# One core's linear attention with a four-expert MoE: a new hand-written order for the first two token tiles, 17 filler groups for five, and one q piece moved from GpSimd to VectorE

## The chip, the core and the metric

The kernel runs on one core of a Trainium2 chip. The core has five engines that run side by side, each through its own instructions in a fixed order: TensorE (PE in the profile, and PEld for its weight loads), VectorE (DVE), ScalarE (ACT), GpSimd (POOL) and SyncE (SP). SP, ACT and POOL also issue the DMA transfers of this kernel. An engine stops at an instruction until the semaphores that it waits for are set, and whatever stands behind it on the same engine waits with it.

The metric is the device time of one execution in microseconds (us). The runs of the kernel before gave 484.59, 484.69 and 487.03; the median is 484.69.

## What is computed

```python
def phi(x): return np.where(x > 0, x, np.exp(x) - 1.0) + 1.0
# q, k, v: 8 batches x 8 heads x 576 rows x 64, fp32
kv  = einsum('bhsd,bhse->bhde', phi(k), v)
z   = sum(phi(k), axis=2)
x   = (phi(q) @ kv) / (phi(q) @ z + 1e-6)      # linear attention
x   = x.transpose(0, 2, 1, 3).reshape(4608, 512)
p   = domain_probs / (domain_probs.sum(-1) + 1e-9)
out = sum over 4 experts e of p[:, e] * (relu(x @ w1[e]) @ w2[e])
# w1[e]: 512 x 1024, w2[e]: 1024 x 512
```

The result has 4608 x 512 numbers in fp32. Nearly all of the arithmetic lies in the two layers of the four experts.

## The kernel before

The 4608 tokens go through the experts in nine tiles of 512. Tile j takes 512 of the 576 rows of batch j; the ninth tile gathers the 64 rows that each batch leaves over. Attention of a batch has to be done before its tile can enter layer 1, so the batches behind the first are prepared while PE works on the experts of the tile ahead of them. Only batch 0 has nothing ahead of it.

The kernel writes the order of its instructions itself. Every piece of work is a generator with a name, put into a list with a position. `CFG["EARLY"]` is a list of names written by hand; `advance` (L1126) takes them one by one and runs the generator of that name up to its next `yield`, which emits its instructions. A name stands as often in the list as its generator has parts. What EARLY does not name follows in the order of positions. EARLY covers batch 0, the whole of tile 0, the preparation of batch 1 and most of tile 1. As each engine runs its instructions in the order in which they were emitted, EARLY is the order of all engines and of the DMA queues.

The names that the change and the prediction touch:

- `lq`, `lk`, `lv` load the four pieces of q, k and v of batch 0 (L568, L560). k and v pieces hold two heads with all their rows; q piece i holds half of the heads and half of the rows. A piece is 256 or 288 KB. There are three slots for raw q, so `lq1` waits until one is free.
- For phi: `qe` and `ke` are the exps on ACT (L601, L583), `ql` and `kl` compute max(x + 1, 1) (L604, L586), `qm` and `km` the minimum of both on DVE (L607, L590). CFG["QL"] names the engine of each `ql`, V for DVE and P for POOL.
- `vc` casts v to fp16 (L593); by CFG["VC"] = 'PVAP' pieces 0 to 3 are cast on POOL, DVE, ACT and POOL.
- `qT` transposes q on PE (L615) and copies it on ACT (L617). `kv` is the product of k and v (L626, 18 matmuls for a pair of heads) and two copies into kvz (L637, on ACT or DVE). `nd` computes numerators and denominators (L648) and divides on DVE (L651, L652). `xT` transposes the result (L662) and copies it (L664).
- `L` is one part of expert 0's layer 1 for tile 0 (L675) with its ReLU on ACT (L684).
- `warm` emits fillers (L1016): matmuls of zeros, 128x512, whose result nobody reads. CFG["WARM"] gives the number of matmuls in each `warm`.
- `w1er` and `w2er`, such as w131 or w231, load half r of expert e's weights for layer 1 or 2 (L247 and L241, 512 KB; expert 0's layer 1 comes in four quarters of 256 KB, L244). All of them are issued by POOL. `k0` to `q3` load pieces of batch 1 (L339), and `rk`, `rv` half of its left-over rows (L317), also on POOL. `b1.loadlq` loads the left-over rows of q on SP, in two transfers of 64 KB, and `b1.load1` another k piece ahead of them.
- `p1` to `p7` and `c22` are block products of layer 1 of the other experts and tiles, in Strassen-Winograd form (L887): p1.021 is tile 0, expert 2, half 1. They need the sums of weight blocks `s` (DVE, L765 to L771) and of x blocks `ts` (L868; ts0 on DVE, ts1 and later ones on POOL).
- `ye.xx` is a quarter of layer 2 of expert e for 128 tokens of tile 0 (L735); `m` are the layer 2 products of the later tiles (L830), `hs` and `t` the sums that they need (POOL L797 to L803, DVE L782 to L788).

A POOL weight load has to wait for the landing of the load eight places ahead of it in POOL's own row of loads; in the trace POOL stands still for this several times between 18 and 43 us.

Of the kernel before, what the change touches and what calls it, by code (L numbers as in the profile page):

```python
# [91 lines left out]
    "LV": 'SSSS',  # L92
    "KL": 'VVVV',
    "VC": 'PVAP',
    "QL": 'VVPV',
    "QT": 'AAAA',
    "KC": ('AA', 'AV', 'VA', 'AA'),
    "XT": ('AA', 'AA', 'AV', 'AV'),
    "CUT": (((0, 2, 4),) * 4, ((0, 2, 4),) * 4),
    "MOVE": {"m73.10": 512.0, "m73.11": 512.0, "m73.20": 512.0, "m73.21": 512.0, "m72.41": 528.0},  # L100
    "WARM": (14, 3, 2, 1, 5),
    "BANK": {'qT0': 'py', 'qT1': 'b', 'nd00': 'py', 'nd00+': 'b', 'kv2': 'py', 'xT00': 'b', 'kv3': 'b', 'nd10+': 'b', 'L00': 'b', 'L10': 'py', 'nd01': 'b', 'xT01': 'py', 'nd11+': 'b', 'L20': 'e', 'L30': 'e', 'L01': 'e', 'L11': 'py', 'L21': 'py', 'L31': 'b', 'b1.qT3': 'py', 'b1.nd30': 'py', 'b1.nd21': 'b', 'b1.q1': 'b', 'b1.qT1': 'py', 'b1.nd01': 'py', 'b1.xT2': 'b', 'b1.nd11': 'py', 'b1.xT0': 'b'},
    "EARLY": (
# [31 lines left out]
    ),  # L135
}

# [1032 lines left out]
```

## Time and profile before

| | us |
|---|---|
| median of three runs | 484.69 |
| profiled execution | 484.06 |
| its span, first to last instruction | 482.3 |
| around the span | 1.8 |
| PE busy | 474.5 (98%) |
| PEld busy (overlaps PE) | 407.4 (84%) |
| DVE busy | 377.6 (78%) |
| POOL busy | 356.1 (74%) |
| ACT busy | 331.4 (69%) |

The profile is one execution, taken by the hardware profiler. A row of a timeline gives the start in us from the span's beginning, the time that the instruction or the run of instructions took, the engine, the line of the kernel, the operation, the tile it writes and the tiles it reads, sizes, and how many instructions are in the run (x8). In brackets stands the idle time of the engine just before it and what ended that idle time: [0.49 <-DVE vpos L593] means that the engine stood still for 0.49 us until DVE had written vpos at line 593. Instructions of one engine overlap by some tens of ns up to 0.2 us, so the time from one start to the next is the price of one in a row, and not the time that it took itself.

A row of the busy time by stretches gives the stretch, its length, then for PE, PEld, DVE, ACT and POOL the busy time with the number of instructions, the granted clock of TensorE (1.00 is full), the mean busy share of the core's DMA engines, and GB/s.

### The profile page before, as it was taken

To read this page: it belongs to the slowest core of one execution; us is meant where nothing else is said; L and a number is where in the kernel's file an instruction comes from. 1 tells how busy PE (TensorE), PEld (TensorE's weight loads), DVE (VectorE), ACT (ScalarE), POOL (GpSimd) and SP (SyncE) were. 2 spreads that over 40 slices of the span, in tenths; PEclk is the share of its full clock that TensorE was granted. 3 is DMA by queue.
4 is the path that set the end of the run, shared out by engine and by line. 5 is a ranking of instruction groups with operands and counts; after the bars stand their busy time and mean duration, and the time that the engine had idled before them with its cause. 6 is when DMAs were issued, how large, how long until landed. Compare 5 with 4: busy or idle time off the path is not lost.

```text
span 482.3 us, 12013 instructions
## 1 busy us (share of the span) xinstructions
PE 474.5 (98%) x4565; PEld 407.4 (84%) x4565; DVE 377.6 (78%) x794; ACT 331.4 (69%) x662; POOL 356.1 (74%) x340
## 2 busy tenths in 40 slices
PE   7999999999999999999999999999999999999997
PEld 3766766898889888998889888988898888888886
DVE  5778988997868895889679885988787756775677
ACT  4689989956895599649874888478954465446540
POOL 5566044789866986789777977697769877987775
PEclk9999999999999999999999999999999999999999
DMA  8999986442445154533552436323230020003002
GB/s 292 219 218 256 232 212 210 124 112 83 135 140 115 39 160 154 119 59 117 173 134 62 112 123 170 78 73 112 65 68 12 2 88 2 0 1 89 2 1 87
DMA packets 80025, 53.67 MB, mean 111 GB/s; under 512 B 45088, under 2 KB 72736, under 8 KB 79968
## 3 DMA queue, kind: packets, MB, share of 16 engines
q1 hardware_dynamic: 69920, 40.56, 30.6%
q0 software_dynamic: 8800, 11.27, 12.1%
q10 hardware_dynamic: 1248, 1.08, 0.7%
q8 instruction: 35, 0.57, 0.5%
q14 instruction: 22, 0.18, 0.1%
HBM read 45.16 MB, written 9.44 MB: 113 GB/s over the span
## 4 chain that ended last, share of the span: by engine, by line
PE 96%; DVE 1%; DMA 1%; issue 0%; ACT 0%; SPq 0%; DVEq 0%
PE py L830 39%; PE pb L887 25%; PE pe L887 19%; PE py L735 6%; PE ph L675 1%; PE psum_nd L492 1%; PE psum_kv L464 1%; DMA rawq<-in_q_dram 1%; PE pb L830 1%; PE pe L830 1%; DVE kpos L586 0%; PE psum_nl L510 0%; PE psum_num L648 0%; PE psum_xh L662 0%; DVE qp L607 0%
## 5 line engine op out<-in xcount | busy, mean ns | idle before, releaser
L726 DVE SCALAR_TENSOR_TENSOR acc<-py,p_sb,acc 128x256 f32<-128x256 f32 (+1 forms) x382 | 182.3, 489 | 42.3 <-PE py L830 38.3
L871 DVE CUSTOM_DVE_ANT_0 h<-pe,u 128x512 f16<-128x512 f32 x140 | 96.2, 689 | 45.5 <-PE pe L887 27.8
L887 PEld LDWEIGHTS <-w 128*128 128x128 f16 x1120 | 108.9, 98 | 16.2
L797 POOL TENSOR_TENSOR hs<-h 128x512 f16<-128x512 f16 x64 | 74.6, 1165 | 56.9 <-DVE h L871 52.8
L830 PEld LDWEIGHTS <-h 128*128 128x128 f16 x1024 | 99.6, 98 | 11.5
L830 PE MATMUL py<-w,h 128*128 128x256 f16 x744 | 106.4, 273 | 0.0
L898 ACT COPY u<-pb 128x512 f32<-128x512 f32 x140 | 82.5, 592 | 29.9 <-PE pb L887 27.8
L799 POOL TENSOR_TENSOR hs<-hs,h 128x512 f16<-128x512 f16 x64 | 73.9, 1155 | 26.3 <-PE py L830 23.8
L887 PEld LDWEIGHTS <-s 128*128 128x128 f16 x840 | 81.2, 98 | 12.0 <-DVE s L767 0.2
L887 PE MATMUL pb<-tt,w 128*128 128x256 f16 x560 | 83.9, 273 | 0.0
L830 PEld LDWEIGHTS <-hs 128*128 128x128 f16 x768 | 74.5, 98 | 8.8 <-issue 0.2
L803 POOL TENSOR_TENSOR hs<-h,hs 128x512 f16<-128x512 f16 x64 | 74.4, 1162 | 0.9 <-PE py L830 0.7
L830 PE MATMUL py<-t,hs 128*128 128x256 f16 x496 | 74.1, 273 | 0.0
L801 POOL TENSOR_TENSOR h<-h 128x512 f16<-128x512 f16 x64 | 73.9, 1154 | 0.1
L920 ACT ACTIVATE h<-pe 128x512 f16<-128x512 f32 x70 | 42.0, 601 | 41.3 <-PE pe L887 40.7
L913 ACT COPY pe<-pb 128x512 f32<-128x512 f32 x70 | 40.0, 572 | 42.0 <-PE pb L887 15.8
L941 ACT ACTIVATE h<-pb 128x512 f16<-128x512 f32 x70 | 41.9, 601 | 6.0 <-PE pb L887 5.9
L887 PE MATMUL pe<-tt,s 128*128 128x256 f16 x280 | 42.0, 273 | 0.0
L887 PE MATMUL pb<-tt,s 128*128 128x256 f16 x280 | 41.8, 273 | 0.0
L887 PE MATMUL pe<-xT,s 128*128 128x256 f16 x248 | 37.1, 273 | 0.0
L887 PE MATMUL pb<-xT,w 128*128 128x256 f16 x248 | 37.1, 273 | 0.0
L830 PE MATMUL py<-w,hs 128*128 128x256 f16 x248 | 37.0, 273 | 0.0
(132 smaller groups left out, 594.4 us busy)
## 6 DMA issues: line engine op xcount, KB each, us to landing
w<-in_moe_w_dram POOLq DMA_DIRECT2D x14, 512.0 KB, 10.6
out_dram<-acc SPq DMA_DIRECT2D x28, 256.0 KB, 2.6
rawb<-in_k_dram SPq DMA_DIRECT2D x24, 256.0 KB, 3.0
rawb<-in_q_dram SPq DMA_DIRECT2D x24, 256.0 KB, 2.7
rawb<-in_v_dram SPq DMA_DIRECT2D x24, 256.0 KB, 2.7
out_dram<-acc SPq DMA_DIRECT2D x12, 128.0 KB, 2.4
w<-in_moe_w_dram POOLq DMA_DIRECT2D x4, 256.0 KB, 5.5
rawb<-in_k_dram POOLq DMA_DIRECT2D x4, 256.0 KB, 10.4
```

Source lines behind the costliest of these rows:

```text
L726: nc.vector.scalar_tensor_tensor(out=acc, in0=ps, scalar=pscal, in1=acc, op0=AO.mult, op1=AO.add)
L797: nc.gpsimd.tensor_tensor(out=hs[0], in0=a21, in1=a22, op=AO.add)
L799: nc.gpsimd.tensor_tensor(out=hs[1], in0=hs[0], in1=a11, op=AO.subtract)
L801: nc.gpsimd.tensor_tensor(out=a21, in0=a11, in1=a21, op=AO.subtract)
L803: nc.gpsimd.tensor_tensor(out=hs[3], in0=a12, in1=hs[1], op=AO.subtract)
L830: nc.tensor.matmul(out=ps, lhsT=lhsT(k), rhs=rhs[:, k], start=first and k == 0, stop=k == FH - 1, skip_group_check=True,)
L871: nc.vector._custom_dve(TENSOR_ADD_SAT, out=out, in0=ps, in1=u, s0=BIG, s1=0.0)
L887: nc.tensor.matmul(out=ps[:, kk], lhsT=lk(kc), rhs=rhs[:, kc], start=first and kk == 0 and kc == 0, stop=kc == 1, skip_group_check=True,)
L898: nc.scalar.copy(u, self.b)
L913: nc.scalar.copy(self.e5, self.b)
L920: nc.scalar.activation(self.h[:, :, 0, 0:NH], self.e5, AF.Relu)
L941: nc.scalar.activation(self.h[:, :, 1, 0:NH], self.b, AF.Relu)
```

## The change

Three entries of CFG are altered, and nothing else.

QL gives the third q piece's `ql` to DVE instead of POOL. WARM turns five filler groups with 25 matmuls into one group of 13 and 16 single ones, 29 in all. EARLY goes from 713 to 736 names in a new order. At its head ql3, ql2, qe3, qe2, qm3 and qm2 now come ahead of the work on piece 0; the weight loads w110 to w211 are named sooner among the steps of batch 0; and w231 stands behind w230 and ts1.0, in the rows in which tile 1's first products stand.

POOL's loads in the order in which they are issued:

```
before: w100 w102 w103 w101 w110 w111 k3 w200 rk1 w201 v0 rv0 rk0 v1 rv1 w120 w121 w210 w211 v2 k0 k2
        q1 k1 v3 q0 w130 w131 q3 w220 q2 w221 w231 w230
after:  w100 w102 w101 rv0 w103 w110 w111 w200 rk1 w201 rk0 k3 k2 w120 w121 k1 k0 w210 v2 w211 rv1 v1 v0
        q0 q1 v3 w130 w131 w220 w221 q3 q2 w230 (ts1.0) w231
```

DVE's operations from the first q piece on, by line of the kernel before, with the piece:

```
before: 604 q0, 604 q3, 607 q0, 586 k0, 590 k0, 607 q2, 586 k1, 590 k1, 607 q3, 593 v1, 586 k2, 586 k3, 637, 651, 652, 590 k2, 590 k3
after:  604 q3, 604 q2, 607 q3, 607 q2, 604 q0, 586 k0, 607 q0, 586 k1, 590 k0, 593 v1, 590 k1, 586 k2, 586 k3, 637, 590 k2, 590 k3, 651, 652
```

On POOL the L604 of q2 is gone. On ACT the exps of q3 and q2 stand ahead of that of q0, where those of q2 and q3 stood between and behind the exps of k0 and k1. On PE the first rows are, before: 14 fillers, qT0, 3, qT2, 2, kv0, 1, kv1, nd01, 5; after: 13 and 5 fillers, qT0, 2, qT2, 3, kv0, 2, kv1, 2, nd01, 2, nd00.

The diff, with the first six rows of EARLY and those that name w130 to w231 or p1.101:

```diff
-    "QL": 'VVPV',
+    "QL": 'VVVV',
...
-    "WARM": (14, 3, 2, 1, 5),
+    "WARM": (13,) + (1,) * 16,
...
-        "lq2 lq3 lq0 lk0 qe0 ql0 ql3 qm0 kl0 lk1 lpr0 ke0 km0 qe2 ql2 qm2 lv0 ke1 kl1 km1 warm0 qT0 lv1 lk2 qe3 qm3 warm1 qT2 qT0 vc0 w100 warm2 kv0 vc1 qT2",
-        "warm3 kv1 lk3 kv0 kv0 kl2 kv1 kl3 w102 kv1 nd01 lv3 nd01 warm4 xT11 xT01 ke2 km2 qT3 w103 vc3 lv2 ke3 vc2 nd00 w101 km3 xT01 w110 xT11 w111 kv3 k3 kv2",
-        "qT3 lq1 nd00 qe1 xT00 w200 kv3 rk1 ql1 kv3 kv2 w201 qm1 L01 kv2 nd11 xT10 L31 qT1 v0 nd11 rv0 xT00 xT10 L10 xT21 rk0 xT21 v1 xT31 L11 qT1 xT31 nd10",
-        "L01 L01 rv1 L31 w120 nd10 ts0.2 L00 ts0.0 xT30 ts0.1 xT20 L31 s0.0 L20 xT20 L30 xT30 L10 L10 L00 L00 L30 ts0.3 L30 p1.011 s1.0 p1.010 L11 L20 p1.010",
-        "p2.010 s1.1 L20 w121 p2.010 p1.011 L21 L21 L21 s1.2 p6.010 p5.010 w210 L11 s1.3 p6.011 y0.30 p2.011 p6.010 p7.010 w211 p7.010 s0.1 p6.011 c22.010 v2",
-        "y0.31 y0.00 p4.010 p2.011 y0.32 y0.33 p5.011 b1.k3 k0 pr0 y0.33 t0.0 t0.1 b1.km3 p7.011 p7.011 c22.011 y0.01 y0.02 y0.03 p4.010 b1.lk y0.20 y0.03 k2",
...
-        "s2.1 p2.020 s2.3 s2.2 y0.23 b1.v1 q0 t0.2 p6.020 p6.020 y0.13 p6.021 y0.13 y1.20 p7.020 y1.21 p2.020 p5.020 p7.020 w130 p2.021 y1.22 y1.23 t1.0 y1.10",
-        "w131 p5.021 b1.v2 q3 b1.lkm y1.11 p6.021 b1.k0 b1.k2 b1.k1 w220 t1.1 t1.2 p7.021 y1.12 p7.021 c22.020 p3.020 y1.23 b1.v3 b1.km0 p4.020 p4.020 y1.00",
...
-        "p1.030 b1.qm1 b1.qT1 y1.32 y1.03 b1.qm0 s3.0 p1.031 w231 b1.qT0 s3.1 p2.030 y1.33 p6.030 b1.kv b1.qT0 p6.031 p2.031 b1.nd00 b1.nd01 b1.q3 p6.030 s3.3",
...
-        "b1.xT1 p3.030 b1.nd21 y2.03 b1.xT0 b1.nd20 b1.nd21 y2.23 y2.10 y2.11 ts1.0 p1.101 p1.101 b1.load5 t1.3 b2.load0 t2.0 b1.xT2 y2.12 y2.13 b1.xT2 b2.k1",
...
+        "lq2 lq3 warm0 ql3 ql2 lk0 qe3 qe2 lq0 qe0 qm3 qm2 ql0 lk1 lpr0 lv0 kl0 qm0 kl1 ke0 ke1 lv1 warm1 km0 warm2 warm3 warm4 warm5 qT0 warm6 lk2 warm7 qT2",
+        "vc0 warm8 warm9 warm10 w100 lk3 lv3 w102 w101 rv0 vc3 w103 vc1 km1 w110 w111 kv0 qT2 warm11 w200 rk1 w201 rk0 k3 k2 w120 w121 kl2 k1 k0 w210 kl3 lv2",
+        "v2 w211 rv1 v1 v0 q0 q1 v3 warm12 w130 ke2 lq1 kv1 warm13 kv0 kv0 ke3 kv1 qT0 vc2 warm14 kv1 nd01 warm15 km2 km3 nd01 warm16 nd00 qT3 kv2 xT11 qT3 qe1",
+        "xT01 nd00 xT10 kv3 xT11 xT01 ql1 qm1 kv2 xT00 L11 L01 kv2 xT10 kv3 kv3 nd11 nd11 L21 qT1 xT00 L00 xT31 xT21 xT21 xT31 L20 qT1 nd10 ts0.2 nd10 ts0.0",
+        "s1.0 ts0.1 L01 L11 L01 L21 xT20 L31 xT30 xT20 xT30 L30 L30 L00 L21 L30 L00 L31 L31 L20 p1.011 p1.011 L20 p1.010 s1.1 ts0.3 s1.2 L10 p2.011 s1.3 pr0",
+        "s0.0 p1.010 L10 p2.010 p2.011 L11 L10 p5.011 p2.010 p6.011 p6.010 p6.011 p6.010 y0.20 y0.21 y0.30 p7.010 p5.010 p7.010 b1.lk y0.31 p7.011 y0.22 y0.32",
+        "p4.010 y0.23 p7.011 t0.0 c22.010 w131 w220 y0.33 b1.k2 p4.010 p3.010 y0.23 c22.011 b1.lkm p3.010 p3.011 p4.011 p3.011 y0.33 p4.011 s2.0 s2.1 s2.2 s2.3",
...
+        "b1.xT3 y2.10 p1.101 y2.11 t2.0 b1.qTl b1.load5 b2.load0 w230 ts1.0 w231 b2.lk b1.xT2 p1.100 b1.xT3 b2.k0 p1.101 ts1.1 ts1.2 b2.ones ts1.3 b2.load4",
...
```

45 rows, old and new, of the table nl are left out of this document.

## The prediction

> **What bounds the kernel now.** I read first the busy time by stretches, then what PE waited for, then the timelines of DVE, ACT, POOL and PE up to 75 us.
>
> ```profile
> 8.00:12.00 4.00, 2.71 (x49) 1.42 (x48) 3.90 (x8) 2.81 (x8) 3.98 (x6) 1.00 1.09 367
> 12.00:16.00 4.00, 2.99 (x62) 2.04 (x62) 3.20 (x9) 3.17 (x8) 4.00 (x7) 1.00 1.24 205
> ...
> 24.00:120.00 96.00, 96.00 (x856) 73.63 (x855) 82.81 (x164) 79.92 (x163) 55.42 (x58) 1.00 0.80 182
> 120.00:478.00 358.00, 358.00 (x3489) 320.48 (x3488) 277.49 (x592) 237.22 (x469) 286.72 (x258) 1.00 0.30 82
> ```
>
> After the length of each stretch come PE, PEld, DVE, ACT and POOL busy, then the granted clock, the DMA share and GB/s. From 24 to 478 us PE is busy without a gap and at full clock. The change leaves PE's real matmuls as they are, so it can win time only before about 17 us, where PE waits or runs fillers, and it can lose time wherever a new order makes PE wait.
>
> ```profile
> PE psum_qT L615 <- DVE qp L607: 1.4, 2, 0.7
> ...
> PE psum_num L648 <- DVE kvz L637: 0.8, 1, 0.8
> PE psum_kv L626 <- DVE vpos L593: 0.5, 1, 0.5
> PE psum_xh L662 <- DVE x_sb L652: 0.3, 1, 0.3
> ```
>
> Four links of PE's start wait for DVE, 1.4 + 0.8 + 0.5 + 0.3 = 3.0 us in all. DVE itself:
>
> ```profile
> 6.22 0.76 DVE L604 TENSOR_SCALAR qp<-rawq 128x512 f16<-128x512 f32 x2 [3.71 <-DMA rawq<-in_q_dram]
> 6.90 0.42 DVE L607 TENSOR_TENSOR qp<-ee,qp 128x512 f16<-128x512 f16 x1
> 7.23 0.45 DVE L586 TENSOR_SCALAR kpos<-kraws 128x576 f16<-128x576 f32 x1
> 7.79 0.94 DVE L590 TENSOR_TENSOR kpos<-kexp,kpos 128x576 f16<-128x576 f16 x1
> 8.66 0.41 DVE L607 TENSOR_TENSOR qp<-ee,qp 128x512 f16<-128x512 f16 x1
> 8.99 0.57 DVE L586 TENSOR_SCALAR kpos<-kraws 128x576 f16<-128x576 f32 x1
> 9.66 0.46 DVE L590 TENSOR_TENSOR kpos<-kexp,kpos 128x576 f16<-128x576 f16 x1
> 10.04 0.42 DVE L607 TENSOR_TENSOR qp<-ee,qp 128x512 f16<-128x512 f16 x1
> 10.37 0.75 DVE L593 CAST vpos<-vraws 128x576 f16<-128x576 f32 x1
> 11.04 1.33 DVE L586 TENSOR_SCALAR kpos<-krawt 128x576 f16<-128x576 f32 x2
> 12.40 0.23 DVE L637 CAST kvz<-psum_kv 64x65 f16<-64x65 f32 x1
> ...
> 13.27 0.69 DVE L652 TENSOR_TENSOR x_sb<-psum_num,recip 128x512 f16<-128x512 f32 x1
> 13.88 0.81 DVE L590 TENSOR_TENSOR kpos<-kexp,kpos 128x576 f16<-128x576 f16 x2
> ```
>
> It idles 3.71 us for the first raw q and then has no gap from 6.22 to 12.6 us. Each link that PE waits for stands somewhere in this row of operations.
>
> **The change at the start.** Pieces 2 and 3 of q, which DVE now handles behind piece 0, come first in the new order. That they land before 6.22 is seen on POOL, which begins piece 2 at 4.33 the moment its load is there:
>
> ```profile
> 4.33 1.92 POOL L604 TENSOR_SCALAR qp<-rawq 128x512 f16<-128x512 f32 x1 [2.90 <-DMA rawq<-in_q_dram]
> 7.76 0.66 POOL L593 CAST vpos<-vraws 128x576 f16<-128x576 f32 x1 [1.50 <-DMA vraws<-in_v_dram]
> ```
>
> ```profile
> 6.22 0.63 ACT L601 ACTIVATE ee<-rawq 128x512 f16<-128x512 f32 x1 [3.06 <-DMA rawq<-in_q_dram]
> ```
>
> So three operations leave DVE's gapless row for its idle time: the second L604 (0.34, half of 6.22 to 6.90) and two L607 (0.33 each, 8.66 to 8.99 and 10.04 to 10.37), 1.00 us together. The L604 that QL takes from POOL (1.92 there, 0.34 on DVE) lies in the idle 3.71 as well. ACT loses two exps from its run that begins at 6.22 (0.63 each) into its own idle 3.06.
>
> In the new order DVE runs from 6.22: L604 0.34, L586 0.34, L607 0.33, L586 0.57, so L590 of k piece 0 starts at 7.80, as before, and ends its slot at 8.67. Behind it now come the cast of v piece 1 (0.67, 10.37 to 11.04) to 9.34, L590 of piece 1 (0.38) to 9.72, two L586 (1.36) to 11.08 and L637. So L637 starts 1.3 us sooner than 12.40. Then both L590 of the later pieces (0.81) stand ahead of L652, which stood ahead of them: L637's 0.2 and 0.81 bring L652's pair to about 12.1, where the 13.03 to 13.27 of before becomes 12.1 to 12.3. The first x_sb is 1.0 us sooner. I take **-1.1** for PE's start, between 1.0 and 1.3. The bounds: -0.3, if only the last of the four waits goes, because L590 of k piece 0 does not move; -1.9, if besides the 1.00 that L590 loses its excess (0.94 - 0.46 = 0.48, it runs beside POOL's cast at 7.76) and the links on ACT follow with another 0.4.
>
> On that L590: by the Trainium skill, SBUF — State Buffer, Who interferes with whom, a DVE operation with two SBUF inputs and a GpSimd operation that reads SBUF exclude each other, and whoever is first holds on for its whole length. If DVE is first by a hair in the new order, L590 is 0.48 shorter and POOL's cast later instead, which the sum would carry as -1.5 rather than -1.1. The row 7.79 0.94 beside 9.66 0.46 fits it.
>
> **Fillers.** 25 become 29, five groups become one of 13 and 16 singles.
>
> ```profile
> 11.18 0.48 PE L626 MATMUL psum_kv<-vpos,kpos 64*64 64x65 f16 x18 [0.49 <-DVE vpos L593]
> ...
> 12.85 1.24 PE L1016 MATMUL warm_ps<-qz 128*128 128x512 f16 x5
> ```
>
> One costs 0.23 us (12.85 to 14.02 for five, the row behind it starts there), four more 0.9. I cost them at 0: the 3.0 us of waits cover them, the last of them stands ahead of the first nd00, and what PE waits for comes from DVE. Without that cover they cost 0.9.
>
> On their spread: by the Trainium skill, TensorE: Matmul & The Clock Gate, Part 1, the clock falls to half after a window of some 3.4 us with too little work. By the Trainium skill that would cost here some 2 us of matmuls at half speed, if singles were too thin. The row 8.00 to 12.00 shows PE busy 2.71 of 4.00 with clock 1.00, and in the new order 13 and five singles stand ahead of the first transposes, so I give it nothing.
>
> **Expert weights of layer 1.** POOL's DMA order changes: expert 2's and 3's pieces move, and four b1 pieces pass expert 1's. All pieces are one stream, near 210 GB/s from 24 to 60 us:
>
> ```profile
> GB/s 292 219 218 256 232 212 210 124 112 83 135 140 115 39 160 154 119 59 117 173 134 62 112 123 170 78 73 112 65 68 12 2 88 2 0 1 89 2 1 87
> ```
>
> The tightest piece of before is expert 3's second half of layer 1 (w131). DVE waits for its landing until 51.74, PE reads it at 52.48:
>
> ```profile
>   DMA w<-in_moe_w_dram: 1.0, 1
> ```
>
> ```profile
> 51.74 0.69 DVE L765 TENSOR_TENSOR s<-w 128x1024 f16<-128x1024 f16 x1
> ```
>
> ```profile
> 52.48 0.60 PE L887 MATMUL pe<-xT,w 128*128 128x256 f16 x4
> ...
> 60.83 1.03 PE L735 MATMUL py<-w,h 128*128 128x512 f16 x4
> ...
> 71.75 0.59 PE L735 MATMUL py<-w,h 128*128 128x512 f16 x2
> ```
>
> The same POOL pieces stand ahead of w131 in both orders, so it cannot land sooner. Two 64 KB pieces of left-over q on SP now come before it, since the k pieces that free their way are handled sooner: 128 KB at 218 GB/s is 0.60 us, landing 51.65 + 0.60 = 52.25 (I put the landing 0.1 ahead of 51.74). Counted in the two orders, PE has one group of four 128x256 matmuls more ahead of it (0.43). PE wants it at 52.48 - 1.1 + 0.43 = 51.81: a stall of **+0.44**, that is, at most 0.66 of the 1.1 pass this point (bounds 0 without the two pieces, 1.3 with -1.9 won before). w221 follows with one piece between: 52.25 + 2 x 2.4 (512 KB at 218 GB/s) = 57.1, and is wanted at 60.83 - 0.66 - 2.85 (work that moved behind it) = 57.3: no stall.
>
> **Expert 3's last piece, w231.** Before, POOL issues it as the last of three, by 47.5; now ts1.0 (L868), which waits for tile 1's x, stands ahead of it:
>
> ```profile
> 45.19 2.29 POOL L241 DMA_DIRECT2D w<-in_moe_w_dram  x3
> 64.36 1.16 POOL L868 TENSOR_TENSOR tt<-xT 128x512 f16<-128x512 f16 x1 [16.89 <-ACT xT L536]
> ```
>
> So it is issued at 64.36 + 1.16 - 0.66 = 64.9. No row shows a 512 KB piece with an empty queue. From below, 256 KB took 5.5 (first row); from above, L247 took 6.7 at least and L241 8.9 at least (the rows behind it):
>
> ```profile
> w<-in_moe_w_dram POOLq DMA_DIRECT2D x4, 256.0 KB, 5.5
> ```
>
> ```profile
> DMA to landing us min/median/max: 6.7/8.6/10.5
> ```
>
> ```profile
> DMA to landing us min/median/max: 8.9/12.9/17.3
> ```
>
> It lands at 70.4 to 73.8, by 6.7 at 71.6. I take 6.7, as its queue is shorter than that of any of these. PE reads it first at 71.75 in before and, with 0.12 more work ahead, at 71.87 less what is still won. So this piece lets 0.3 of the win pass.
>
> **Small stalls.** ACT and DVE have little air where the order is new:
>
> ```profile
> 50.00:60.00 10.00, 10.00 (x92) 7.64 (x90) 9.58 (x23) 9.81 (x22) 0.00 (x0) 1.00 1.20 229
> ```
>
> ACT 9.81 and DVE 9.58 of 10.00 while PE is never stopped: a different order costs between 0 and, with three misses of one 128x512 step on ACT (0.4 us, the spacing of PE's groups), 1.2. I take **+0.4** up to w231, where 0.3 of the win may pass anyway, and **+0.2** behind it in tile 1's layer 2.
>
> **Sum.** -1.1 + 0.44 + 0.4 = -0.26 at w231, whose bound (-0.3) then costs nothing; +0.2 behind it: -0.06. Profiled execution 484.06 (span 482.3 and 1.8 around it) to 484.0. The median of before, 484.69, lies 0.63 above that execution; with it the forecast is **484.6**, no change.
>
> **Rivals.** (a) The win stays: no stall at w131 and w231, because the two q pieces or the shorter queue cost less than I put. Then 484.69 - 1.1 = 483.6, with -1.9 482.8. For it: PE's four waits are real. Against: w131's wait on DVE in before shows the stream at its limit. (b) Slower: w231, issued behind ts1.0, takes as long as L241's rows. Landing at 64.9 + 8.9 = 73.8 costs 73.8 - 71.87 = 1.9, with the median 12.9 it costs 5.9: 486.6 to 490.6. It decides once the piece lands behind 71.9. For it: every L241 row; against: those had four pieces ahead. (c) The change does not do what it says: L590 of k piece 0 stays at 7.8, and with it every later link; 0.3 won, 0.4 + 0.2 and no w131 stall: 485.0.
>
> **How the numbers follow.** My forecast 0.40, (a) 0.22, (b) 0.20, (c) 0.18. About 0.5%, 2.4 us, is what a measurement of this kernel can tell from no change: 482.3 to 487.1. Faster beyond that needs more than -1.9: 0.05. Slower needs (b) with more than 9.4 us: 0.16, and 0.03 for stalls of several kinds: 0.19. Same 0.76. The range goes from (a)'s end, 482.8, to (b) with 9.7 us, 487.4; the forecast's own is 483.6 to 485.6.
>
> **What would show it.** In the changed kernel's profile: L604 on DVE at about 4.4 twice; L637 on DVE near 11.1; the first layer 1 matmul 1.0 sooner; a PE wait of about 0.4 for w131 near 52; POOL's w231 issue near 65 and its first reader near 71.6. I am wrong if PE waits for w231 longer than 1 us, if the first x_sb isn't sooner, or if PE shows waits of over 1 us on ACT or DVE behind 24 us.

## The result, and the profile after

The changed kernel takes 487.60 us (median of 13 runs, 487.39 to 489.00) beside 484.68 for the kernel before on the same chips (13 runs); the ratio is 1.0055, 95% interval 1.0043 to 1.0067. The forecast was 484.6 with a range from 482.8 to 487.4, so the time lies above the range. The profiled execution took 487.54 with a span of 485.8, 3.5 more than the span of before.

The busy time by stretches of the changed kernel, in the columns of before (length, PE, PEld, DVE, ACT, POOL, clock, DMA share, GB/s):

```profile
8.00:12.00 4.00, 3.69 (x59) 2.09 (x58) 2.83 (x8) 3.37 (x9) 4.00 (x6) 1.00 1.08 370
12.00:16.00 4.00, 2.88 (x62) 2.19 (x61) 3.44 (x9) 2.47 (x7) 4.00 (x7) 1.00 1.24 212
24.00:120.00 96.00, 93.78 (x825) 70.47 (x824) 82.18 (x160) 76.62 (x154) 52.80 (x54) 1.00 0.79 174
120.00:478.00 358.00, 357.89 (x3486) 320.09 (x3484) 276.53 (x590) 241.21 (x478) 287.71 (x259) 1.00 0.31 84
```

Between 24 and 120 us PE now stands idle for 2.2 us, where it had no idle time at all. What PE waited for, in us altogether, times, longest:

```profile
PE pe L888 <- DVE h L872: 1.9, 2, 1.2
...
PE psum_xh L663 <- DVE x_sb L653: 1.1, 2, 0.6
PE psum_qT L616 <- DVE qp L608: 0.7, 1, 0.7
PE psum_num L649 <- DVE kvz L638: 0.3, 1, 0.3
```

The waits of the start shrank from 3.0 to 2.1 us. A new one stands at the top: PE waits for DVE's relu-and-add (h, L872), which frees the PSUM bank of an expert product. The lines of the changed kernel are one further on than those of before.

To see where the time went, one needs PE's waiting and its fillers together. The table gives, at a moment t, t less the work that PE has done by then; the work is the sum of the usual spacings (0.11 us for a 128x256 matmul, and so on) of the real matmuls begun, taken from the traces. A number that grows by 0.4 from one row to the next means 0.4 us lost between them. The runs e7 and e11 are told below.

```
t (us)   before   changed   e7      e11
 16      14.12    13.48     13.36   13.46
 28      14.30    14.26     13.62   13.60
 50      14.85    14.81     14.17   14.14
 65      14.88    14.82     14.69   14.37
 80      15.33    15.88     15.27   14.96
 85      15.47    16.09     15.28   14.97
 95      15.53    17.49     15.34   15.03
105      15.54    18.61     15.35   15.04
140      16.14    19.73     15.95   15.64
```

The changed kernel is 0.64 us ahead at 16 us and has given this back by 28. It is level with before until 65 us, loses 0.6 by 80, 2.5 from there to 105 and 0.5 by 140.

### The profile page after: what moved, and what is told of

Read it like the earlier page. It is cut to its first block, busy times and chain, and to the rows that moved or that the text cites. A ratio compares the mean times of both kernels' runs of the same rounds, so it can differ in the third digit from the quotient of the medians.

```text
span 485.8 us, 12015 instructions
## 1 busy us (share of the span) xinstructions
PE 476.6 (98%) x4569; PEld 407.5 (84%) x4569; DVE 377.9 (78%) x795; ACT 332.7 (68%) x662; POOL 355.7 (73%) x339
## 3 DMA queue, kind: packets, MB, share of 16 engines
q0 software_dynamic: 8800, 11.27, 12.1%
## 4 chain that ended last, share of the span: by engine, by line
PE 90%; DVE 3%; DMA 3%; ACT 2%; issue 0%; POOL 0%; DVEq 0%
PE py L831 38%; PE pb L888 24%; PE pe L888 18%; PE py L736 4%; DMA w<-in_moe_w_dram 2%; PE ph L676 1%; PE psum_nd L493 1%; DMA krawt<-in_k_dram 1%; PE psum_kv L465 1%; DMA rawq<-in_q_dram 1%; PE pb L831 1%; DVE h L872 1%; PE pe L831 1%; DVE w L789 1%; DVE acc L727 0%; DVE t L787 0%
## 5 line engine op out<-in xcount | busy, mean ns | idle before, releaser
L727 DVE SCALAR_TENSOR_TENSOR acc<-py,p_sb,acc 128x256 f32<-128x256 f32 (+1 forms) x382 | 181.6, 488 | 44.3 <-PE py L831 37.1
L872 DVE CUSTOM_DVE_ANT_0 h<-pe,u 128x512 f16<-128x512 f32 x140 | 95.8, 687 | 46.6 <-PE pe L888 26.3
L888 PE MATMUL pe<-xT,w 128*128 128x256 f16 x248 | 37.1, 273 | 0.0
```

Source lines behind the costliest of these rows:

```text
L727: nc.vector.scalar_tensor_tensor(out=acc, in0=ps, scalar=pscal, in1=acc, op0=AO.mult, op1=AO.add)
L872: nc.vector._custom_dve(TENSOR_ADD_SAT, out=out, in0=ps, in1=u, s0=BIG, s1=0.0)
L888: nc.tensor.matmul(out=ps[:, kk], lhsT=lk(kc), rhs=rhs[:, kc], start=first and kk == 0 and kc == 0, stop=kc == 1, skip_group_check=True,)
```

## Experiments

**What stands in DVE's way between 85 and 105 us.** In the changed kernel's trace PE's longest wait and what DVE does ahead of it look like this (timelines of PE and DVE):

```profile
87.69 0.60 PE L888 MATMUL pe<-xT,w 128*128 128x256 f16 x4
89.51 0.60 PE L888 MATMUL pe<-xT,s 128*128 128x256 f16 x4 [1.22 <-DVE h L872]
```

```profile
85.69 1.61 DVE L789 TENSOR_TENSOR w<-w 128x1024 f16<-128x1024 f16 x1
87.22 0.67 DVE L373 SCALAR_TENSOR_TENSOR qp<-qp,psum_ee 128x512 f16<-128x512 f16 x1
87.82 1.04 DVE L789 TENSOR_TENSOR w<-w 128x1024 f16<-128x1024 f16 x1
88.78 0.68 DVE L872 CUSTOM_DVE_ANT_0 h<-pe,u 128x512 f16<-128x512 f32 x1
```

The relu-and-add stands behind two weight sums of layer 2 (`t`, L789), and these took 1.61 and 1.04 us, where the same operation takes 0.68 elsewhere. At that time POOL runs the hidden sums of tile 1 one after the other (timeline of POOL):

```profile
83.92 1.60 POOL L798 TENSOR_TENSOR hs<-h 128x512 f16<-128x512 f16 x1
85.59 1.15 POOL L800 TENSOR_TENSOR hs<-hs,h 128x512 f16<-128x512 f16 x1
86.71 1.60 POOL L802 TENSOR_TENSOR h<-h 128x512 f16<-128x512 f16 x1
```

The groups of DVE's weight sums from 80 to 110 us, first in the kernel before, then in the changed one (count, then busy time and mean in ns), show that there are nine instead of four, and longer ones:

```profile
L786 DVE TENSOR_TENSOR t<-w,t 128x1024 f16<-128x1024 f16 x2 | 1.8, 878 | 0.0
L784 DVE TENSOR_TENSOR t<-w,t 128x1024 f16<-128x1024 f16 x1 | 1.1, 1139 | 0.0
L788 DVE TENSOR_TENSOR w<-w 128x1024 f16<-128x1024 f16 x1 | 0.7, 684 | 0.0
```

```profile
L787 DVE TENSOR_TENSOR t<-w,t 128x1024 f16<-128x1024 f16 x4 | 4.2, 1051 | 0.0
L789 DVE TENSOR_TENSOR w<-w 128x1024 f16<-128x1024 f16 x4 | 4.0, 999 | 0.0
L785 DVE TENSOR_TENSOR t<-w,t 128x1024 f16<-128x1024 f16 x1 | 1.1, 1089 | 0.0
```

At 0.68 each the nine would take 6.1 us; they take 9.3. The theory was that these late sums make the loss. The rivals were the new order of tile 1's products, and w231. The first run moves four of the sums forward again (fragments of EARLY):

```diff
- m10.21 t0.2 y3.23
+ b1.v3 t0.2 p4.021
...
- p3.110 t0.3 m10.10
+ q2 t0.3 b1.kv
...
- p2.111 t1.2 b2.qm3
+ t1.1 t1.2 b1.qm3
...
- p7.120 t1.3 b2.nd1
+ b1.next t1.3 b1.load0
```

> The changed kernel with four weight sums of layer 2 (t0.2, t0.3, t1.2, t1.3, all on DVE) taken from behind the first hidden sum of tile 1 (82 to 98 us) to between 45 and 70 us, where the kernel before had them; all else as changed. Theory T (DVE's t sums run beside POOL's hidden sums, take 1.0 to 1.6 us instead of 0.68, and make DVE's relu-and-add late, so PE waits 1.22 and 0.72 us at 89 and 95): those two waits go, 487.6 - 2.0 to - 2.6 = 485.0 to 485.6. Rival R (the new order of products and hidden sums in tile 1 makes PE wait whatever DVE's sums do): 487.3 to 487.8. Rival W (w231 behind ts1.0 is late and pushes all that follows): 487.3 to 487.8, since w231 stays.

It took 488.00 us (ratio to before 1.0057, 1.0043 to 1.0071): no gain. The expected fall didn't come. The two waits for h near 90 and 96 us are down to 0.4 each, but PE now waits in three other places, at 48.0, 62.5 and 63.7 us (for acc, qp and h), in the stretch into which the sums had gone and where the changed kernel has no such wait:

```profile
PE pe L888 <- DVE h L872: 1.2, 3, 0.4
...
PE psum_qT L449 <- DVE qp L373: 0.4, 1, 0.4
PE py L736 <- DVE acc L727: 0.3, 1, 0.3
```

The second run does the reverse in the kernel before:

```diff
- q0 t0.2 p6.020
+ b2.load7 t0.2 p1.111
...
- p1.020 t0.3 s2.1
+ hs10.03 t0.3 hs10.12
...
- t1.1 t1.2 p7.021
+ m10.11 t1.2 p5.110
...
- b1.load5 t1.3 b2.load0
+ m10.31 t1.3 m10.31
```

> The kernel before with one edit: the same four weight sums t0.2, t0.3, t1.2, t1.3 moved behind its first hidden sum of tile 1. Theory T: 484.7 + 1.5 to 3 = 486.2 to 487.7, with t sums of 1.0 to 1.6 us and PE waiting for DVE's relu-and-add between 85 and 105 us. Rivals R and W: no change, 484.4 to 485.0.

488.33 us, ratio 1.0067 (1.0049 to 1.0085): four sums put behind the first hidden sum cost the kernel before as much as the whole change did. PE waits for DVE's sum of the expert outputs (acc), and DVE is at sums again (PE, then DVE):

```profile
88.76 0.60 PE L829 MATMUL py<-t,hs 128*128 128x256 f16 x4 [1.17 <-DVE acc L725]
94.79 0.60 PE L829 MATMUL py<-w,h 128*128 128x256 f16 x4 [1.62 <-DVE acc L725]
```

```profile
84.96 2.76 DVE L785 TENSOR_TENSOR t<-w,t 128x1024 f16<-128x1024 f16 x2
...
92.71 1.63 DVE L787 TENSOR_TENSOR w<-w 128x1024 f16<-128x1024 f16 x1
```

To see whether the first run had only put the sums in a bad place, the next one put the same four where DVE had stood idle in the changed kernel's trace, or into the place of t0.1, which moves ahead with t0.2:

```diff
- c22.021 t0.1 b1.v0
- m10.21 t0.2 y3.23
+ t1.0 t0.1 t0.2 p1.020
...
- p3.110 t0.3 m10.10
+ s0.3 t0.3 b1.km1
...
- p2.111 t1.2 b2.qm3
- p7.120 t1.3 b2.nd1
+ b2.km0 t1.2 t1.3 p6.101
```

> The changed kernel with the four late weight sums placed by hand where DVE stood idle in its trace: t0.1 and t0.2 behind t1.0 (idle 2.05 us at 41), t0.3 where t0.1 stood, t1.2 and t1.3 behind b2.km0 (idle 1.44 us at 72, POOL idle too). The run with the sums at 45 to 70 us gave 488.0, with new waits of 0.5 us where they went in. Theory T2 (DVE is short of time from 40 to 105 us; the changed order leaves it idle for 5 us before 80 and pays with the sums behind it): PE's waits of 1.4 and 0.9 us at 89 and 95 go and no new ones come: 487.6 - 1.5 to - 2.3 = 485.3 to 486.1. Rival R (the order of products and hidden sums in tile 1 makes the waits whatever DVE's sums do): 487.2 to 488.2.

486.72 us, ratio 1.0045 (1.0033 to 1.0057): 0.9 faster than the changed kernel, less than expected. The waits near 89 and 95 are down to 0.41 each, and no new one of that size came (the largest other one behind 24 us is the 0.3 for w231). For the rest, the sums t2.3, t3.3 and t3.1 were moved behind the relu-and-add that they held up:

```diff
- y3.13 t2.3 b2.qm2 t3.3 c22.110
+ c22.110 t2.3 t3.3 m10.11
...
- b1.nl t3.1 c22.111
+ c22.111 t3.1 m10.60
```

> The run with the weight sums in DVE's gaps (486.7), and t2.3, t3.3 and t3.1 besides moved behind the relu-and-add of their neighbourhood (c22.110, c22.111). In the trace of that run PE still stood 0.57 us at 88.9 and at 94.5 for that relu-and-add, which stood on DVE behind sums of 1.37, 1.04 and 1.09 us. Theory T2 (all of PE's loss from 85 to 105 us is DVE's sums standing ahead of the relu-and-add): both go, 485.4 to 486.0. If the order of tile 1's products sets them: 486.5 to 487.0.

487.68 us, ratio 1.0058 (1.0041 to 1.0075): slower again by 1.0. PE no longer waits for h, but for what now stands behind the sums: acc L727, 1.5 us in two waits. So this expectation failed. In this run the operation behind the sums decided what PE waits for, and not whether it waits. Two runs then asked what makes DVE late there. One leaves the late sums out:

```diff
     def weight_sums2(e, part):
+        if (e, part) in [(0, 2), (0, 3), (1, 2), (1, 3), (2, 2), (2, 3), (3, 1), (3, 2), (3, 3)]:
+            return
```

> The changed kernel without the nine weight sums of layer 2 that its order puts behind the first hidden sum of tile 1 (t0.2, t0.3, t1.2, t1.3, t2.2, t2.3, t3.1, t3.2, t3.3); they are left out of the computation, and five of the sum blocks are zeros written by POOL. If DVE's sums make all of the 2.5 us from 85 to 105: PE has no waits there, 487.6 - 2.5 = 485.1 (484.9 to 485.4). If the order of tile 1's products makes half of it, as the run with four sums moved leaves open: 486.1 to 486.6, with waits of 0.4 to 0.6 us near 89 and 95.

The other keeps all nine sums at their late places, and lets POOL write zeros in place of its additions, so that it reads nothing:

```diff
     def hidden_sum(h, hs, i, light):
+        def add(out, in0, in1, op):
+            if light:
+                nc.gpsimd.memset(out, 0.0)
+            else:
+                nc.gpsimd.tensor_tensor(out=out, in0=in0, in1=in1, op=op)
...
+            def hsum(d, i, hT=h, hss=hss, light=j == 1 and e < 2):
```

> The changed kernel with POOL's hidden sums of tile 1, experts 0 and 1, replaced by writing zeros to the same places, so that POOL reads nothing there; this leaves these sums out of the computation, and all of DVE's late weight sums stay where the change puts them. If the sums are long because POOL reads beside them: they take 0.68 us instead of 1.04 to 1.61, DVE has 3.2 us more from 82 to 95, and PE's waits at 89 and 95 fall from 2.3 us to below 0.7: 485.2 to 486.2. If only their number counts: sums still above 1 us, or at 0.68 with the waits left, 487.0 to 487.8.

Without the late sums: 485.47 us, ratio 1.0019 (1.0008 to 1.0029). With the sums and without POOL's reads: 485.94, ratio 1.0027 (1.0018 to 1.0036). The stretch from 80 to 100 us in the changed kernel, without the sums, and without POOL's reads, one fence each:

```profile
80.00:100.00 20.00, 18.06 (x179) 15.18 (x173) 19.51 (x33) 16.59 (x35) 16.39 (x13) 1.00 0.53 148
```

```profile
80.00:100.00 20.00, 19.95 (x194) 17.09 (x189) 14.11 (x29) 16.84 (x36) 16.33 (x15) 1.00 0.59 167
```

```profile
80.00:100.00 20.00, 19.95 (x203) 17.07 (x196) 18.39 (x37) 17.06 (x36) 5.36 (x11) 1.00 0.61 167
```

PE's idle time falls from 1.94 to 0.05 us in both, and the waits for h are gone. In the last run the groups of the nine sums read

```profile
L789 DVE TENSOR_TENSOR w<-w 128x1024 f16<-128x1024 f16 x4 | 2.7, 682 | 0.0
L787 DVE TENSOR_TENSOR t<-w,t 128x1024 f16<-128x1024 f16 x4 | 2.7, 681 | 0.0
L785 DVE TENSOR_TENSOR t<-w,t 128x1024 f16<-128x1024 f16 x1 | 0.7, 684 | 0.0
```

0.68 each, at the same places. So neither the number of the sums nor the order of the products alone makes PE wait there; it takes the late sums together with POOL's reads, which make each of them 0.36 us longer in the mean ((9.3 - 6.1) / 9). The mean hides two kinds: in the changed kernel five of the nine, which started while an addition of POOL was running, took 1.04 to 1.61 us; the other four took 0.67 to 0.68, three of them with an addition of POOL that started after them. The memsets also end sooner than the additions, 0.52 us instead of 1.15 to 1.60, so that POOL is idle for most of the time; but four sums (at 82.96, 89.43, 90.42 and 91.57 us) ran with a memset beside them and still took 0.68. By the measure of the table both runs still lose about 0.5 us more than before between 80 and 105 us, so that some 2 of the 2.5 are accounted for; the rest of what they keep above before, 1.0 and 1.5 us in the medians, stands between 65 and 80 and behind 105. That POOL's reads make the sums longer is the rule of the Trainium skill, SBUF — State Buffer, Who interferes with whom: a DVE operation with two SBUF inputs contends with a GpSimd instruction that reads SBUF, not with one that only writes it. The trace agrees on both halves: up to 1.61 us beside POOL's additions, 0.68 beside its memsets.

**w231.** It was put ahead of ts1.0:

```diff
- w230 ts1.0 w231
+ w230 w231 ts1.0
```

> The changed kernel with w231 issued ahead of ts1.0 instead of behind it, all else as changed. In the changed kernel's trace the piece was issued at 65.08 and landed at about 72.4, and PE stood 0.24 us for it. Rival W (w231 is what made it slower): 487.6 - 2 or more. If it is only these 0.24 us: 487.2 to 487.6, and less still if DVE's later waits take it up.

487.45 us, ratio 1.0062 (1.0046 to 1.0078), not to be told from the changed kernel. In that one the piece was issued at 65.08, and the row of that single load is

```profile
DMA to landing us min/median/max: 7.4/7.4/7.4
```

so it landed at 72.4; PE read it at 72.49 and had stood 0.24 us for it. The rival that made w231 the cause of a slow result falls.

**The order at 72 us.** One run keeps the changed order up to the first p1.100; behind it follow, in the order of before, all names that are not used up by then:

```diff
- b1.nd30 y2.33 b1.xT2 p1.100 p3.031 p3.030
+ b1.nd30 y2.33 b1.xT2
...
```

> The changed kernel's order up to the first product of tile 1 (p1.100, about 72 us), then the order of the kernel before for all that is left, so that the pending t sums come at once and w231 ahead of ts1.0. If all the loss lies in the part behind 72 us (theory T or rival R): 484.7 + 0.3 (what the changed kernel had lost at 70 us) = 484.6 to 485.4. If the loss is a matter of what stands before 72 us: 486.5 to 487.6.

488.35 us, ratio 1.0065 (1.0048 to 1.0081). It answers nothing about the loss behind 72 us, since the two orders don't fit at the joint: PE waits 1.7 us for u and 1.0 for xT, both on ACT, between 69 and 78 us.

**What the start is worth.** The next run keeps QL, WARM and the changed order up to the first step of layer 1; behind it follow again the names not used by then, in the order of before:

```diff
- kv2 xT00 L11 L01 kv2
+ kv2 xT00
...
```

> The changed kernel's entries QL and WARM and its order up to the first step of layer 1 (L11), then the order of the kernel before for all that is left. If the start alone is worth what the changed kernel's trace shows at 16 us (0.64 us less waiting and filling than before) and the order of before keeps it: 484.7 - 0.6 = 484.1. If that lead is lost again because the DMA stream or ACT sets the pace from 18 to 28 us whatever the order: 484.5 to 484.9. If the start cannot be joined to the other order: above 485.0.

493.75 us, ratio 1.0177 (1.0159 to 1.0196). ACT stands 9 us for a v piece of batch 1, which the changed order of POOL's loads brings later than the order of before wants it (timeline of ACT):

```profile
43.73 0.62 ACT L377 COPY vp<-rawv 128x512 f16<-128x512 f16 x1 [8.99 <-DMA rawv<-in_v_dram]
```

Up to 35 us, however, the lead of 0.6 was kept. So the same was tried with POOL's loads in the order of before:

```diff
- w100 ... w102 w101 rv0 vc3 w103 vc1 km1 w110 w111 kv0
+ w100 ... w102 w103 w101 vc3 w110 vc1 km1 w111 k3 kv0
```

> The changed kernel's QL, WARM and order up to the first step of layer 1, but with POOL's loads in the order of the kernel before, and then all the rest in the order of before. The run with the changed loads stood 7.3 us at 45 us and had still 0.58 us of lead at 35 us. If the lead of the start (0.6 us) is real and only the loads broke it: 484.7 - 0.6 = 484.1 (483.9 to 484.3). If before's DMA stream sets the pace and takes the lead (w131 had 0.8 us to spare in it): 484.4 to 484.9.

484.45 us, ratio 0.9994 (0.9985 to 1.0004). The table shows that the lead, 0.68 at 28 and 50 us, shrinks to 0.2 by 65. PE, then DVE at that place:

```profile
53.15 1.05 PE L887 MATMUL pb<-tt,s 128*128 128x256 f16 x8 [0.31 <-DVE s L767]
```

```profile
51.68 0.69 DVE L765 TENSOR_TENSOR s<-w 128x1024 f16<-128x1024 f16 x1 [0.60 <-DMA w<-in_moe_w_dram]
```

PE's own read of w131, at 51.81, does not wait; what it waits for is DVE's sum of it. DVE waits for w131 until 51.68, as before until 51.74, however early PE is. Another 0.5 us goes at 344 us, where PE waits for ACT's acc in this trace and not in that of before. The next run has one more edit, the late k minima behind the first division:

```diff
- nd01 warm15 km2 km3 nd01 warm16
+ nd01 warm15 nd01 km2 km3 warm16
```

> The same with one more edit: the minima of the late k pieces (km2, km3) behind the division of the first x (nd01) on DVE, as in the kernel before, where the changed kernel has them ahead of it, and where they took 1.29 us beside POOL's cast. If it is these two that ate the lead at 12 to 14 us: x_sb 0.9 us sooner, PE 0.3 to 0.8 us further ahead: 483.3 to 483.8. If the late k pieces are then missing for the second pair of kv: as the run before it or slower, 484.1 to 484.7.

484.48 us, ratio 0.9989 (0.9977 to 1.0000). The first x_sb came at 12.31 instead of 13.12, as expected, and PE was no further ahead at 16 us (13.41 in the table's measure, beside 13.36). Now kv2 waits for its k, and the second x_sb sets PE's pace:

```profile
13.42 0.47 PE L626 MATMUL psum_kv<-vpos,kpos 64*64 64x65 f16 x18 [0.38 <-DVE kpos L590]
14.64 0.40 PE L662 MATMUL psum_xh<-identh,x_sb 128*128 128x128 f16 x4 [0.52 <-DVE x_sb L652]
```

Two runs go after w131, on top of e7. First other work for PE while DVE makes the sums of it:

```diff
- y1.33 p6.030 b1.kv b1.qT0 p6.031 p2.031 b1.nd00
+ y1.33 p2.031 p6.030 b1.kv b1.qT0 p6.031 b1.nd00
```

> The run with the new start, POOL's loads of before and the order of before (484.45, a lead of 0.68 us at 50 us of which 0.47 were lost at 53 us), with p2.031, which needs w131 itself, ahead of p6.030, which needs the sums that DVE makes of it. If what takes the lead is that PE gets to p6.030 ahead of the sums, 0.43 us of other work there: 484.0 to 484.2. If PE then waits for w131 itself or for ACT's copy of p1.031: 484.3 to 484.6.

484.13 us, ratio 0.9985 (0.9975 to 0.9995). PE no longer waits for the sum, but the interval overlaps with that of e7, so the gain in time is not shown. Then, with the swap kept, fewer bytes beside w131:

```diff
- w131 ... b1.load1 ... b1.loadlq
+ w131 b1.loadlq ... w230 b1.load1
...
-                (bt if m < len(mine) else nxt).load(*later[m])
+                (bt if m < len(mine) else nxt).load(*later[m], eng=nc.gpsimd if first and m == len(mine) + 1 else nc.sync)
...
-        put_at(CFG["PR"][3], "b1.loadlq", b1.load_left, "q")
+        put_at(CFG["PR"][3], "b1.loadlq", lambda: b1.load_left("q", eng=nc.gpsimd))
```

> The same as the run with the swap, and the three transfers that SP starts at 44.5 us (b1.load1 of 256 KB, b1.loadlq of 2 x 64 KB) issued by POOL behind w230 and behind w131. If the DMA stream sets w131's landing (384 KB fewer beside it), DVE's sums of it start 0.6 to 1.5 us sooner than in the run without, near 50.5 instead of 51.7, and the lead holds: 483.9 to 484.2. If w131's landing does not move: as the run with the swap.

483.97 us, ratio 0.9982 (0.9972 to 0.9993): faster than the kernel before by 0.7 us, though not to be told from the run with the swap alone. DVE has no wait for w131 any more and starts on it at 50.96 instead of 51.68:

```profile
50.96 0.68 DVE L765 TENSOR_TENSOR s<-w 128x1024 f16<-128x1024 f16 x1
```

**Fillers.** e7 without its 16 single fillers:

```diff
-    "WARM": (13,) + (1,) * 16,
+    "WARM": (13,) + (0,) * 16,
```

> The run with the new start, POOL's loads of before and the order of before (484.45), with the 16 single fillers left out, so that only the first 13 are left; what is computed stays. If fillers lie in PE's waits and cost nothing: 484.2 to 484.7. If they cost their 0.22 us each outside the waits: up to 3.5 us less, 481 to 484. If PE's clock falls without them (busy share in 8 to 16 us from 0.97 down to about 0.5): granted clock below 1.00 in the stretch from 7 to 20 us and 485.5 to 488.

485.46 us, ratio 1.0011 (0.9999 to 1.0023), 1.0 above e7 in the medians and 0.8 by the ratios. Three stretches, with PE's busy time, clock, DMA share and GB/s:

```profile
5.67:9.08 3.41, 1.72 (x29) 1.00 1.06 406
9.08:19.32 10.24, 8.24 (x111) 0.50 1.18 248
19.32:24.00 4.68, 4.68 (x53) 1.00 1.14 235
```

The granted clock is 0.50 from 9.08 to 19.32 us, three times 3.41 us, and 1.00 again behind that. In the 3.41 us ahead of the fall PE was busy for 1.72, with waits of 1.05 and 0.64 us where the fillers had been. By the Trainium skill, TensorE: Matmul & The Clock Gate, Part 1, an idle window of some 3.4 us brings half the clock. The trace agrees on the half and on the length; the window in it was not idle, but busy for half of its time.

## Why the prediction failed, by its own steps

- **What bounds the kernel** was right: PE, with something to win only ahead of 17 us. The changed kernel lost what it lost wherever its order made PE wait. One of the prediction's own signs of being wrong came: a wait of over 1 us on DVE behind 24 us (1.22, at 89.5).
- **The start, -1.1,** had the right sign; it was 0.64 at 16 us. L637 came at 11.30 (11.08 was forecast), held not by DVE's own row but by 0.76 us of waiting for ACT's kvz; the pair of L590 that now stands ahead of the division took 1.29 us instead of 0.81, beside POOL's second v cast at 11.57, which the forecast had left out, and x_sb came at 13.12 instead of 12.1:

```profile
11.30 0.23 DVE L638 CAST kvz<-psum_kv 64x65 f16<-64x65 f32 x1 [0.76 <-ACT kvz L638]
11.55 1.29 DVE L591 TENSOR_TENSOR kpos<-kexp,kpos 128x576 f16<-128x576 f16 x2
...
13.12 0.69 DVE L653 TENSOR_TENSOR x_sb<-psum_num,recip 128x512 f16<-128x512 f32 x1
```

Run e8 shows that this term did not decide: with x_sb at 12.31 PE was no earlier, for kv2's k and the second x_sb were the links. The changed kernel then lost the 0.6 between 16 and 28 us, through its own order of layer 1; e7, with the order of before from there, did not.
- **L590 of k piece 0** took 0.45 instead of 0.94: DVE was first (7.76, POOL's cast 7.86), as the sentence on the Trainium skill allowed, and POOL's cast took 0.88 instead of 0.66. This did not reach PE: DVE's next operation, the cast of v piece 1, then stood 0.36 us for its load.
- **Fillers at nothing:** no run takes only the four additional ones away, so that price stays not shown. That the singles are not too thin was right: with them the clock stayed at 1.00, and without them it falls (e12), at a cost of 0.8 to 1.0 us and not some 2.
- **w131, +0.44:** the piece came later by about what was forecast, for DVE's wait for it ended at 52.50 instead of 51.74:

```profile
52.50 0.69 DVE L766 TENSOR_TENSOR s<-w 128x1024 f16<-128x1024 f16 x1 [0.20 <-DMA w<-in_moe_w_dram]
```

PE read it at 52.88, near the 52.48 and the 0.43 of additional work that the prediction counted, with no lead taken off, and did not wait. So it cost nothing, because no lead was left by then. Where the lead was kept (e7) 0.47 were lost near this place, but that this is so close to 0.44 is luck: the landing had not moved there, and PE waited for DVE's sum of the piece and not for the piece. e11 shows that the bytes beside it set its landing, as the prediction had it. The stream's rate was misread: the row of GB/s has 218, 256 and 232 in its slices from 24 to 60 us and not some 210; at 232 the 0.60 would be 0.56, and nothing hangs on that.
- **w231** was issued at 65.08 (64.9 forecast), took 7.4 (6.7) and cost 0.24. As a bound it was harmless, and as rival (b) it was the wrong mechanism for a slow result: e6.
- **Small stalls: the step that failed.** The +0.4 up to w231 stands beside the 0.6 lost between 16 and 28 us and the 0.6 between 65 and 80, of which 0.24 are w231's own. The "+0.2 behind it in tile 1's layer 2" stands beside 2.5 from 80 to 105 us and 0.5 by 140. It was taken as a lump from how busy ACT and DVE were, without asking which of DVE's operations had been moved to where. The edit takes five weight sums that stood between 36 and 76 us to the stretch of POOL's hidden sums, nine instead of four; there they took 9.3 us instead of 6.1 and held up DVE's relu-and-add, for which PE waited 1.9 us. The prediction had in hand both the row that showed the effect (7.79 0.94 beside 9.66 0.46) and the rule of the Trainium skill, and used them on one operation of the start alone. The profile of before shows a late sum of over 1 us as well (1139 ns in the groups above).
- **The other rivals:** (a), the win stays, fell with the order of layer 1; (c) was right that L590 of k piece 0 stays at 7.8 (7.76), and wrong that every later link stays with it: L637 came 1.1 us sooner, and the lead at 16 us was 0.64 and not 0.3.
- **Left open:** the 0.5 from 105 to 140 us and most of the 0.6 from 65 to 80 weren't tried, nor the some 0.5 that e13 and e14 leave between 80 and 105.

The expected gain of 1.1 came out as 0.64, was gone by 28 us, and would not have reached the end whole: in e7, where it was kept, only 0.2 of it passed DVE's sum of w131.

## What to carry to other kernels

When an order is changed, list for each engine which operations changed places, and ask for each what the neighbour engine runs at its new place: in this case a two-input DVE operation beside POOL's additions took 1.04 to 1.61 us instead of 0.68 where POOL was first, and PE paid for it by waiting for what stood behind it on DVE. A wait that disappears when an operation is moved may come back behind the next one; to tell whether the order or the load is at fault, take the load away (e13) and the disturbance away (e14) one at a time. A lead won at the start can be lost again at the first transfer that can't land sooner; find that one first.

## What the runs showed of the hardware

- 128x1024 f16 additions on DVE took 0.68 us with POOL idle or writing only. Beside POOL's additions five of nine took 1.04 to 1.61, and those of POOL went from 1.15 to as much as 1.60.
- Without the single fillers PE was busy for 1.72 of 3.41 us, and then the granted clock was 0.50 for 10.24 us. In the kernel before PE was busy for 2.02 of 3.41 us from 5.88 to 9.29 us, and the clock stayed at 1.00; with the 16 single fillers (e7) it stayed at 1.00 too.
